# Column rings and 64-column pieces (24 KB per descriptor) in a DMA-bound grouped 1x1 convolution

## The chip, the cores and the metric

One core of a Trainium2 chip. Times are device microseconds (us) of that core.

## The reference

`x` is 512 x 512 pixels of 192 channels in bf16, in four groups of 48 channels. Each group is multiplied by its own 48 x 48 matrix:

```python
xg = x.reshape(B, H, W, G, Cg)                      # k = 1, so no padding and one tap
out = einsum('bhwgc,gcd->bhwgd', xg, w[0, 0])       # G = 4, Cg = 48
return out.reshape(B, H, W, C)                      # bf16
```

100.7 MB are read and 100.7 MB written; the arithmetic is small.

## The kernel before

Pixels are taken as 2048 columns of 128 (one pixel per partition). In one DMA each partition holds `s` neighbouring pixels, so one partition's share is one contiguous run of `s` x 384 B in memory: 12 KB at 32 columns. There are six input and six output buffers of 32 columns. The work goes in groups of 4 columns: TensorE transposes six 128 x 128 tiles into PSUM, VectorE copies them to SBUF (`ev1`), TensorE multiplies by the weights, and ScalarE copies the result to the output buffer; in every third group VectorE takes half of that (`ev2`). The code is cut, and its comments are added here:

```python
PPC = 32
HEAD = (4, 4, 8, 16)            # small pieces first, so that work starts early
TAIL = (16, 8, 4, 4)            # and last, so that it ends early
NBI = 6
NBO = 6
...
        @block.sync                                   # the load queue
        def _(sp):
            ...
            for n in range(n_chunks):
                if n >= NBI:
                    wq.wait(t_done, chunk_g1[n - NBI])        # that buffer has been transposed
                b = n % NBI
                sp.dma_start(x_sb[b][:, 0:sizes[n] * C], rows_view(xf, n)).then_inc(ld_sem[b], 16)
...
        @block.scalar                                 # ScalarE: copies, and the store queue
            def store(n):
                act.dma_start(rows_view(of, n), o_sb[b][:, 0:sizes[n] * C]).then_inc(st_sem[b], 16)
            for g in range(NG):
                n, lg = groups[g]
                if lg == 0:
                    wait_out_free(wq, n)                      # the store of n - 6 has landed
                wq.wait(mm_done, g + 1)
                while pending and pending[0][1] <= g:         # two groups after the last copy
                    store(pending.pop(0)[0])
                ...                                           # the copy of group g
```

TensorE's steady groups are a loop (`pe.Fori`); the other engines' programs are written out.

Of the kernel before, what the change touches and what calls it, by code (L numbers as in the profile page):

```python
# [6 lines left out]
BF16 = mybir.dt.bfloat16  # L7
# [14 lines left out]
ESHIFT = 112  # L22
ECOLS = 272

PPC = 32
HEAD = (4, 4, 8, 16)
TAIL = (16, 8, 4, 4)
NBI = 6
NBO = 6
NXP = 4  # L30
NOB = 4
LOOK = 3
ST_DELAY = 2
RING = 6


class Waiter:
# [9 lines left out]
        self.eng.wait_ge(sem, val)  # L47


def plan_chunks(npix):  # L50
    assert npix % 512 == 0, "the pixel count must be a multiple of 512"
    cols = npix // 128
    head, tail = list(HEAD), list(TAIL)
    if cols < sum(head) + sum(tail) + PPC:
        head, tail = [], []
    mid = cols - sum(head) - sum(tail)
    first = len(head)
    full = mid // PPC
    sizes = head + [PPC] * full
    if mid % PPC:  # L60
        sizes.append(mid % PPC)
    return sizes + tail, first, full


def bass_standalone__grouped__vision_kernel(nc, x, w, out):
# [1 line left out]
    assert Cx == C and tuple(w.shape) == (1, 1, GROUPS, CG, CG)  # L67
    npix = B * H * W_

    sizes, first_full, n_full = plan_chunks(npix)  # L70
    n_chunks = len(sizes)

    xf = x.rearrange("b h w c -> (b h w) c")
    of = out.rearrange("b h w c -> (b h w) c")
    wv = w.rearrange("a b g c d -> c (a b g) d")

    col0, groups, chunk_g0, chunk_g1, c0 = [], [], [], [], 0
    for n, s in enumerate(sizes):
        col0.append(c0)
        c0 += s  # L80
        chunk_g0.append(len(groups))
        groups += [(n, lg) for lg in range(s // 4)]
        chunk_g1.append(len(groups))
    NG = len(groups)

    body = NBI * PPC // 4
    assert body % 12 == 0
    loop_g0 = chunk_g0[first_full]
    reps = max(0, (n_full * PPC // 4 - LOOK) // body)
    loop_g1 = loop_g0 + reps * body  # L90

    def shared(g):
        return g % 3 == 1 and g < NG - 3

    dve_prog = [("wcopy", 0)]
    for g in range(NG + LOOK):
# [3 lines left out]
        if 0 <= h < NG and shared(h):  # L100
            dve_prog.append(("ev2", h))

    def rows_view(ap, n):
        s = sizes[n]
        return ap[128 * col0[n]:128 * (col0[n] + s), :].rearrange("(p i) c -> p (i c)", p=128)

    with ExitStack() as es:
        block = es.enter_context(nc.Block())
        x_sb = [es.enter_context(nc.sbuf_tensor(f"x_sb{i}", [128, PPC * C], BF16)) for i in range(NBI)]
        o_sb = [es.enter_context(nc.sbuf_tensor(f"o_sb{i}", [128, PPC * C], BF16)) for i in range(NBO)]  # L110
        xT_sb = [es.enter_context(nc.sbuf_tensor(f"xT_sb{i}", [128, 2 * UC], BF16)) for i in range(NXP)]
        ident = es.enter_context(nc.sbuf_tensor("ident", [128, 128], BF16))
        esel = es.enter_context(nc.sbuf_tensor("esel", [CG, ECOLS], BF16))
# [5 lines left out]
        def sem(name):  # L119
            return es.enter_context(nc.semaphore(name))  # L120

        ld_sem = [sem(f"ld{i}") for i in range(NBI)]
        st_sem = [sem(f"st{i}") for i in range(NBO)]
        w_sem, id_sem, e_sem, wb_sem, wc_sem = (sem(s) for s in ("w_sem", "id_sem", "e_sem", "wb_sem", "wc_sem"))
        p0_sem, p1_sem = sem("p0_sem"), sem("p1_sem")
        t_done, mm_done = sem("t_done"), sem("mm_done")
# [1 line left out]
        fa_sem = [sem(f"fa_{i}") for i in range(RING)]  # L128
        d2_sem = [sem(f"d2_{i}") for i in range(2)]

        def wait_out_free(wq, n):
            wq.wait(st_sem[n % NBO], 16 * (n // NBO))

        @block.gpsimd
        def _(gp):
# [11 lines left out]
        @block.sync  # L147
        def _(sp):
            wq = Waiter(sp)
            sp.dma_start(w_sb[:], wv).then_inc(w_sem, 16)  # L150
            for n in range(n_chunks):
                if n >= NBI:
                    wq.wait(t_done, chunk_g1[n - NBI])
                b = n % NBI
                sp.dma_start(x_sb[b][:, 0:sizes[n] * C], rows_view(xf, n)).then_inc(ld_sem[b], 16)  # L155

        @block.tensor
        def _(pe):

            def build_weights():  # L160
                pe.wait_ge(e_sem, 1)
                pe.wait_ge(w_sem, 16)
                last = None
                for (tc, r, g, c0_) in WBLOCKS:
                    s0 = ESHIFT - r
                    col = WOFF[tc] + c0_
                    last = pe.matmul(o_ps[:, NOB - 1, col:col + CG], lhsT=esel[:, s0:s0 + 128],  # L167
                                     rhs=w_sb[:, g, :], start=True, stop=True, skip_group_check=True)
                last.then_inc(wb_sem, 1)

            def transposes(g):
                n, lg = groups[g]
                if g == 0:
                    pe.wait_ge(id_sem, 1)
                if lg == 0:
                    pe.wait_ge(ld_sem[n % NBI], 16)
                xb = x_sb[n % NBI]
                ins = []
                for ul in range(2):
                    u = lg * 2 + ul  # L180
                    for tc in range(3):
                        col = u * UC + tc * 128
                        j = ul * 3 + tc
                        ins.append(pe.transpose(xT_ps[:, g % NXP, j * 128:(j + 1) * 128],  # L184
                                                xb[:, col:col + 128], ident[:]))
                if lg == 0:
                    ins[1].then_inc(ld_sem[n % NBI], -16)
                ins[-1].then_inc(t_done, 1)

            def matmuls(g):  # L190
                xs = xT_sb[g % NXP]
                waited = [e1_sem[g % RING]]
                if g == 0:
                    pe.wait_ge(wc_sem, 1)
                if g >= 2:
                    waited.append(fa_sem[(g - 2) % RING])
                    if shared(g - 2):
                        waited.append(d2_sem[(g - 2) // 3 % 2])
                for s in waited:
                    pe.wait_ge(s, 1)  # L200
                ins = []
                for ul in range(2):
                    v = 2 * g + ul
                    for tc in range(3):
                        j = ul * 3 + tc
                        c0_, c1_ = COLR[tc]
                        ins.append(pe.matmul(o_ps[:, v % NOB, c0_:c1_], lhsT=xs[:, j * 128:(j + 1) * 128],  # L207
                                             rhs=wt[:, WOFF[tc]:WOFF[tc] + (c1_ - c0_)],
                                             start=(tc == 0), stop=(tc == 2), skip_group_check=True))
                for i, s in enumerate(waited):  # L210
                    ins[1 + i].then_inc(s, -1)
                ins[-1].then_inc(mm_done, 1)

            def step(g):
                if g + LOOK < NG:
                    transposes(g + LOOK)
                matmuls(g)

            build_weights()
            for g in range(min(LOOK, NG)):  # L220
                transposes(g)
            for g in range(loop_g0 if reps else 0):
                step(g)
            if reps:
                with pe.Fori(0, reps, 1):
                    for g in range(loop_g0, loop_g0 + body):
                        step(g)
            for g in range(loop_g1 if reps else 0, NG):
                step(g)

        @block.vector
        def _(dve):
            wq = Waiter(dve)
            for (op, g) in dve_prog:
                if op == "wcopy":
                    wq.wait(wb_sem, 1)
                    dve.tensor_copy(wt[:], o_ps[:, NOB - 1, 0:WCOLS]).then_inc(wc_sem, 1)  # L237
                    continue
                n, lg = groups[g]
                if op == "ev1":  # L240
                    wq.wait(t_done, g + 1)
                    dve.tensor_copy(xT_sb[g % NXP][:], xT_ps[:, g % NXP, 0:2 * UC]).then_inc(e1_sem[g % RING], 1)  # L242
                else:
                    wait_out_free(wq, n)
                    wq.wait(mm_done, g + 1)
                    u = lg * 2 + 1
                    v = 2 * g + 1
                    dve.tensor_copy(o_sb[n % NBO][:, u * UC:(u + 1) * UC],  # L248
                                    o_ps[:, v % NOB, 0:UC]).then_inc(d2_sem[g // 3 % 2], 1)

        @block.scalar
        def _(act):
            wq = Waiter(act)
            pending = []

            def store(n):
                b = n % NBO
                act.dma_start(rows_view(of, n), o_sb[b][:, 0:sizes[n] * C]).then_inc(st_sem[b], 16)  # L258

            for g in range(NG):  # L260
                n, lg = groups[g]
                if lg == 0:
                    wait_out_free(wq, n)
                wq.wait(mm_done, g + 1)
                while pending and pending[0][1] <= g:
                    store(pending.pop(0)[0])
                v = 2 * g
                ob = o_sb[n % NBO]
                if shared(g):
                    u = lg * 2  # L270
                    ins = act.copy(ob[:, u * UC:(u + 1) * UC], o_ps[:, v % NOB, 0:UC])  # L271
                else:
                    dst = ob[:, lg * 2 * UC:(lg + 1) * 2 * UC].rearrange("p (u c) -> p u c", u=2)
                    ins = act.copy(dst, o_ps[:, v % NOB:v % NOB + 2, 0:UC])  # L274
                ins.then_inc(fa_sem[g % RING], 1)
                if g == chunk_g1[n] - 1:
                    pending.append((n, g + ST_DELAY))
            for (n, _) in pending:
                act.wait_ge(fa_sem[(chunk_g1[n] - 1) % RING], 1)
                store(n)  # L280
            for b in range(NBO):
                cnt = len(range(b, n_chunks, NBO))
                if cnt:
                    wq.wait(st_sem[b], 16 * cnt)


# [26 lines left out]
```

## Time and profile before

| | before |
|---|---|
| time, median (range) of 4 runs | 493.42 us (493.20 to 493.61) |
| span in the profile | 492.4 us |
| TensorE, VectorE, ScalarE busy | 84%, 73%, 70% |
| DMA, mean of the span / slices 5 to 37 | 409 GB/s / 427 to 430 GB/s |
| one 32-column load, issue to landing | 39.2 us (median) |

First the page: the DMA lines of its second part (40 equal slices of the span; the digit is the share of the time in which the 16 DMA engines were busy, in tenths), the queues of the third (q1 is the load queue, q10 the store queue) and the last line of the chain of the fourth.

```profile
DMA  8999999999999999999999999999999999999663
GB/s 294 414 418 425 427 427 429 430 429 429 430 429 429 429 428 427 427 429 427 428 430 429 429 430 430 429 430 427 428 427 429 428 429 429 429 429 427 279 253 143
DMA packets 20386, 201.56 MB, mean 409 GB/s; under 512 B 2448, under 2 KB 3472, under 8 KB 4496
q1 hardware_dynamic: 10288, 100.69, 48.5%
q10 hardware_dynamic: 10080, 100.67, 48.3%
DMA x_sb<-in_x_dram 71%; PE o_ps L207 13%; PE xT_ps L184 10%; ACT o_sb L274 3%; ACTq L258 1%; SPq L155 0%; SPq L150 0%; ACTq L47 0%
```

The DMA engines have work all the time, at 427 to 430 GB/s in the middle. The Trainium skill, page "DMA: Bandwidth & Descriptors", section "Where 436 GB/s comes from", gives 435.2 GB/s as the ceiling of the fabric. The trace fits it: the middle is 1.3% below. (The same section has about 358 GB/s of HBM bandwidth per core as what binds transfers between HBM and SBUF; the 429 measured on this one core are above that.) But the last three slices have 279, 253 and 143 GB/s, and that is a clue. Next, the chain of work that ended last, in order of time (start us, length us, what).

```profile
362.35 39.55 DMA x_sb<-in_x_dram
401.94 0.51 PE xT_ps L184 x6
407.92 39.53 DMA x_sb<-in_x_dram
447.49 0.51 PE xT_ps L184 x6
453.46 28.42 DMA x_sb<-in_x_dram
```

One step from load to load is 45.5 us, and it covers six pieces (the buffer count): 7.6 us for 2 x 1.573 MB, so 414 GB/s. The engines on average move 429. Some engines run ahead of the one that the chain follows.

To see it I worked two things out from the trace; they are no views of the page. A DMA's completion is sixteen separate increments of its semaphore, one for each DMA engine. For each load, the time of the first and the sixteenth:

```
load issued at   first landing   sixteenth   spread
      12.76           33.58        37.11       3.5
     134.73          165.22       174.21       9.0
     271.31          296.89       310.80      13.9
     407.92          428.57       447.45      18.9
     453.46          458.38       481.88      23.5     (the last, 4 columns)
```

Over the 18 loads between the third and the fourth row the first landing comes every 7.32 us, the sixteenth every 7.59. I call the engine that lands last the laggard. Each piece is complete only when it has landed, and by the end it is 20 us behind.

The second: the trace has a record for every DMA packet (start, duration, queue, size; no engine number). A packet starts 3 to 4 ns before the recorded end of the one before it on its engine, and a 4-byte packet follows each eight data packets of a queue, so one engine can be followed packet by packet, back from the last packet of the run. Followed so, the laggard works from its start to 491.3 us without one gap. A packet of 1.5, 3, 6 or 12 KB takes an undisturbed engine (one that shows no extra time) 61.5, 117.5, 230.5 or 456.5 ns from start to start: 4.5 ns plus the bytes at 27.2 B/ns. The laggard's 12 KB packets are recorded at 476 to 478 ns instead of 460.

So the time is the laggard's work and almost nothing else: start, its share of the bytes at the undisturbed rate, and its extra.

### The profile page before, as it was taken

The numbers are of one execution on the slowest core, as the hardware profiler recorded it, in microseconds if no ns is written. First come the engines' busy times: TensorE is split into PE (matmuls) and PEld (weight loads), VectorE is DVE, ScalarE is ACT, GpSimd is POOL, SyncE is SP. The second block draws the span as 40 slices with busy tenths as digits, with TensorE's granted clock in tenths as the row PEclk, the third lists the DMA queues.
The fourth block names the chain that finished last, engine by engine and source line by source line (L and its number), as shares of the span: only waits on it lengthen the run. The fifth ranks groups of instructions, "written<-read, shape, count | busy, mean of one in ns | idle before, by whom it ended". The sixth has DMA issues, their size and how long they took to land.

```text
span 492.4 us, 14343 instructions
## 1 busy us (share of the span) xinstructions
PE 415.0 (84%) x6154; PEld 389.1 (79%) x6154; DVE 358.1 (73%) x683; ACT 345.6 (70%) x513; POOL 1.3 (0%) x8
## 2 busy tenths in 40 slices
PE   5999999998888888888889888888888888888953
PEld 5899999887877877878778778787787787877852
DVE  3888888876777777777778777777677777777750
ACT  2788888876766777667767676776776766766752
POOL 1000000000000000000000000000000000000000
PEclk9999999999999999999999999999999999999996
DMA  8999999999999999999999999999999999999663
GB/s 294 414 418 425 427 427 429 430 429 429 430 429 429 429 428 427 427 429 427 428 430 429 429 430 430 429 430 427 428 427 429 428 429 429 429 429 427 279 253 143
DMA packets 20386, 201.56 MB, mean 409 GB/s; under 512 B 2448, under 2 KB 3472, under 8 KB 4496
## 3 DMA queue, kind: packets, MB, share of 16 engines
q1 hardware_dynamic: 10288, 100.69, 48.5%
q10 hardware_dynamic: 10080, 100.67, 48.3%
q8 instruction: 7, 0.11, 0.1%
q14 instruction: 11, 0.09, 0.0%
HBM read 100.68 MB, written 100.66 MB: 409 GB/s over the span
## 4 chain that ended last, share of the span: by engine, by line
DMA 71%; PE 24%; ACT 3%; issue 1%; ACTq 1%; SPq 0%
DMA x_sb<-in_x_dram 71%; PE o_ps L207 13%; PE xT_ps L184 10%; ACT o_sb L274 3%; ACTq L258 1%; SPq L155 0%; SPq L150 0%; ACTq L47 0%
## 5 line engine op out<-in xcount | busy, mean ns | idle before, releaser
L242 DVE COPY xT_sb<-xT_ps 128x768 bf16<-128x768 bf16 x512 | 283.8, 555 | 114.8 <-PE xT_ps L184 109.7
L274 ACT CAST o_sb<-o_ps 128x768 bf16<-128x768 f32 x342 | 267.0, 799 | 107.9 <-PE o_ps L207 101.6
L184 PE MATMUL xT_ps<-ident,x_sb 128*128 128x128 bf16 x3072 | 257.2, 220 | 58.3 <-DMA x_sb<-in_x_dram 58.3
L207 PE MATMUL o_ps<-wt,xT_sb 128*128 128x144 bf16 (+1 forms) x3072 | 297.4, 233 | 10.4 <-ACT o_sb L274 10.1
L184 PEld LDWEIGHTS xT_ps<-ident,x_sb 128*128 128x128 bf16 x3072 | 195.0, 98 | 70.0 <-DMA x_sb<-in_x_dram 68.9
L207 PEld LDWEIGHTS o_ps<-wt,xT_sb 128*128 128x128 bf16 x3072 | 211.5, 98 | 24.5 <-issue 17.7
L271 ACT CAST o_sb<-o_ps 128x384 bf16<-128x384 f32 x170 | 81.6, 480 | 33.3 <-PE o_ps L207 24.0
L248 DVE CAST o_sb<-o_ps 128x384 bf16<-128x384 f32 x170 | 94.2, 554 | 8.1 <-PE o_ps L207 7.0
L237 DVE CAST wt<-o_ps 128x480 bf16<-128x480 f32 x1 | 0.7, 657 | 3.2 <-PE o_ps L167 3.2
L167 PE MATMUL o_ps<-w_sb,esel 48*128 48x48 bf16 x10 | 0.6, 209 | 2.6 <-DMA w_sb<-in_w_dram 2.6
L167 PEld LDWEIGHTS o_ps<-w_sb,esel 48*128 48x128 bf16 x10 | 0.4, 111 | 2.5 <-POOL esel L139 2.5
L274 ACT ACT_TABLE_LOAD x1 | 1.3, 1283 | 0.8 <-PEq L298 0.8
L139 POOL TENSOR_SCALAR_AFFINE_SELECT esel<-esel 48x272 bf16<-48x272 bf16 x1 | 0.4, 406 | 0.0
L136 POOL MEMSET esel<- 48x272 bf16 x1 | 0.3, 318 | 0.3 <-POOLq L298 0.3
L143 POOL TENSOR_SCALAR_AFFINE_SELECT ident<-ident 128x128 bf16<-128x128 bf16 x1 | 0.3, 285 | 0.0
L137 POOL MEMSET ident<- 128x128 bf16 x1 | 0.2, 198 | 0.0
L298 POOL MEMSET const-bfloat16-1.0<- 128x1 bf16 x1 | 0.1, 102 | 0.0
L298 POOL MEMSET const-uint8-127<- 128x1 uint8 x1 | 0.1, 102 | 0.0
L298 POOL MEMSET const-float32-0.0<- 128x1 f32 x1 | 0.1, 98 | 0.3 <-issue 0.3
L298 POOL MEMSET const-float32-1.0<- 128x1 f32 x1 | 0.1, 98 | 0.0
## 6 DMA issues: line engine op xcount, KB each, us to landing
x_sb<-in_x_dram SPq DMA_DIRECT2D x62, 1536.0 KB, 39.2
out_dram<-o_sb ACTq DMA_DIRECT2D x62, 1536.0 KB, 31.0
x_sb<-in_x_dram SPq DMA_DIRECT2D x2, 768.0 KB, 22.1
out_dram<-o_sb ACTq DMA_DIRECT2D x2, 768.0 KB, 11.7
x_sb<-in_x_dram SPq DMA_DIRECT2D x4, 192.0 KB, 15.5
x_sb<-in_x_dram SPq DMA_DIRECT2D x2, 384.0 KB, 19.8
out_dram<-o_sb ACTq DMA_DIRECT2D x4, 192.0 KB, 6.9
out_dram<-o_sb ACTq DMA_DIRECT2D x2, 384.0 KB, 10.2
```

The costliest lines, as they stand in the source:

```text
L136: gp.memset(esel[:], 1.0).then_inc(p0_sem, 1)
L139: gp.affine_select(out=esel[:], in_=esel[:], pattern=[[-1, ECOLS]], compare_op=AluOpType.is_equal, fill=0.0, base=ESHIFT, channel_multipli ...
L167: last = pe.matmul(o_ps[:, NOB - 1, col:col + CG], lhsT=esel[:, s0:s0 + 128], rhs=w_sb[:, g, :], start=True, stop=True, skip_group_check=True)
L184: ins.append(pe.transpose(xT_ps[:, g % NXP, j * 128:(j + 1) * 128], xb[:, col:col + 128], ident[:]))
L207: ins.append(pe.matmul(o_ps[:, v % NOB, c0_:c1_], lhsT=xs[:, j * 128:(j + 1) * 128], rhs=wt[:, WOFF[tc]:WOFF[tc] + (c1_ - c0_)], start=(tc ...
L237: dve.tensor_copy(wt[:], o_ps[:, NOB - 1, 0:WCOLS]).then_inc(wc_sem, 1)
L242: dve.tensor_copy(xT_sb[g % NXP][:], xT_ps[:, g % NXP, 0:2 * UC]).then_inc(e1_sem[g % RING], 1)
L248: dve.tensor_copy(o_sb[n % NBO][:, u * UC:(u + 1) * UC], o_ps[:, v % NOB, 0:UC]).then_inc(d2_sem[g // 3 % 2], 1)
L258: act.dma_start(rows_view(of, n), o_sb[b][:, 0:sizes[n] * C]).then_inc(st_sem[b], 16)
L271: ins = act.copy(ob[:, u * UC:(u + 1) * UC], o_ps[:, v % NOB, 0:UC])
L274: ins = act.copy(dst, o_ps[:, v % NOB:v % NOB + 2, 0:UC])
L298: nc = _bacc.Bacc("TRN2", target_bir_lowering=False, num_devices=1)
```

## The change

Intent: larger packets, so that the fixed cost of each weighs less, and buffers that are rings of 256 columns, so that pieces of any size fit. VectorE takes its half in every fourth group instead of every third, since the loop is now 64 groups. The core of the diff (cut):

```diff
-PPC = 32
-HEAD = (4, 4, 8, 16)
-TAIL = (16, 8, 4, 4)
-NBI = 6
-NBO = 6
+BIG = 64
+RCOLS = 256
+HEAD = (4, 4, 8, 16, 32)
+TAIL = (32, 16, 8, 4, 4)
-RING = 6
+RING = 8
...
-        return g % 3 == 1 and g < NG - 3
+        return g % 4 == 1 and g < NG - 3
...
-        x_sb = [es.enter_context(nc.sbuf_tensor(f"x_sb{i}", [128, PPC * C], BF16)) for i in range(NBI)]
-        o_sb = [es.enter_context(nc.sbuf_tensor(f"o_sb{i}", [128, PPC * C], BF16)) for i in range(NBO)]
+        x_sb = es.enter_context(nc.sbuf_tensor("x_sb", [128, RCOLS * C], BF16))
+        o_sb = es.enter_context(nc.sbuf_tensor("o_sb", [128, RCOLS * C], BF16))
...
-        def wait_out_free(wq, n):
-            wq.wait(st_sem[n % NBO], 16 * (n // NBO))
+        def wait_out_free(wq, g):
+            if g >= body:
+                p = store_at[g - body]
+                wq.wait(st_sem[p.key], st_val[p])
...
-                if n >= NBI:
-                    wq.wait(t_done, chunk_g1[n - NBI])
-                b = n % NBI
-                sp.dma_start(x_sb[b][:, 0:sizes[n] * C], rows_view(xf, n)).then_inc(ld_sem[b], 16)
+                wq.wait(t_done, p.g1 - body)
+                sp.dma_start(ring_view(x_sb, p), rows_view(xf, p)).then_inc(ld_sem[p.key], 16)
```

More of the change, by code (lines that the diff above doesn't have):

```diff
@@ L47, in wait, with __init__, plan_pieces @@
         self.eng.wait_ge(sem, val)
-def plan_chunks(npix):
-    assert npix % 512 == 0, "the pixel count must be a multiple of 512"
-    cols = npix // 128
-    head, tail = list(HEAD), list(TAIL)
-    if cols < sum(head) + sum(tail) + PPC:
-        head, tail = [], []
-    mid = cols - sum(head) - sum(tail)
-    first = len(head)
-    full = mid // PPC
-    sizes = head + [PPC] * full
-    if mid % PPC:
-        sizes.append(mid % PPC)
-    return sizes + tail, first, full
+class Piece:
+    def __init__(self, col, size, key):
+        self.col, self.size, self.key = col, size, key
+        self.g0, self.g1 = col // 4, (col + size) // 4
+def plan_pieces(cols, head, tail):
+    sizes = list(head) if cols >= sum(head) + sum(tail) else []
+    last = list(tail) if sizes else []
+    mid = cols - sum(sizes) - sum(last)
+    pieces, c = [], 0
+    for s in sizes + [BIG] * (mid // BIG) + ([mid % BIG] if mid % BIG else []) + last:
+        whole = s == BIG and c % BIG == 0
+        pieces.append(Piece(c, s, ("big", c // BIG % (RCOLS // BIG)) if whole else ("own", len(pieces))))
+        c += s
+    return pieces
 def bass_standalone__grouped__vision_kernel(nc, x, w, out):
@@ L68, in bass_standalone__grouped__vision_kernel @@
     npix = B * H * W_
-    sizes, first_full, n_full = plan_chunks(npix)
-    n_chunks = len(sizes)
+    cols = npix // 128
+    assert npix % 512 == 0, "the pixel count must be a multiple of 512"
+    NG = cols // 4
+    loads = plan_pieces(cols, HEAD, TAIL)
+    stores = plan_pieces(cols, HEAD, TAIL)
+    load_of = {p.g0: p for p in loads}
+    store_at = {g: p for p in stores for g in range(p.g0, p.g1)}
+    store_end = {p.g1 - 1: p for p in stores}
     xf = x.rearrange("b h w c -> (b h w) c")
@@ L75, in bass_standalone__grouped__vision_kernel @@
     wv = w.rearrange("a b g c d -> c (a b g) d")
-    col0, groups, chunk_g0, chunk_g1, c0 = [], [], [], [], 0
-    for n, s in enumerate(sizes):
-        col0.append(c0)
-        c0 += s
-        chunk_g0.append(len(groups))
-        groups += [(n, lg) for lg in range(s // 4)]
-        chunk_g1.append(len(groups))
-    NG = len(groups)
-    body = NBI * PPC // 4
-    assert body % 12 == 0
-    loop_g0 = chunk_g0[first_full]
-    reps = max(0, (n_full * PPC // 4 - LOOK) // body)
+    body = RCOLS // 4
+    assert body % RING == 0 and BIG % 4 == 0 and RCOLS % BIG == 0
+    bigs = [p for p in loads if p.key[0] == "big"]
+    loop_g0 = bigs[0].g0 if bigs else 0
+    reps = max(0, (sum(p.size for p in bigs) // 4 - LOOK) // body)
     loop_g1 = loop_g0 + reps * body
     def shared(g):
-        return g % 3 == 1 and g < NG - 3
+        return g % 4 == 1 and g < NG - 3
     dve_prog = [("wcopy", 0)]
@@ L101, in bass_standalone__grouped__vision_kernel, with rows_view, ring_view @@
             dve_prog.append(("ev2", h))
-    def rows_view(ap, n):
-        s = sizes[n]
-        return ap[128 * col0[n]:128 * (col0[n] + s), :].rearrange("(p i) c -> p (i c)", p=128)
+    def rows_view(ap, p):
+        return ap[128 * p.col:128 * (p.col + p.size), :].rearrange("(p i) c -> p (i c)", p=128)
+    def ring_view(t, p):
+        at = p.col % RCOLS
+        assert at + p.size <= RCOLS
+        return t[:, at * C:(at + p.size) * C]
     with ExitStack() as es:
         block = es.enter_context(nc.Block())
-        x_sb = [es.enter_context(nc.sbuf_tensor(f"x_sb{i}", [128, PPC * C], BF16)) for i in range(NBI)]
-        o_sb = [es.enter_context(nc.sbuf_tensor(f"o_sb{i}", [128, PPC * C], BF16)) for i in range(NBO)]
+        x_sb = es.enter_context(nc.sbuf_tensor("x_sb", [128, RCOLS * C], BF16))
+        o_sb = es.enter_context(nc.sbuf_tensor("o_sb", [128, RCOLS * C], BF16))
         xT_sb = [es.enter_context(nc.sbuf_tensor(f"xT_sb{i}", [128, 2 * UC], BF16)) for i in range(NXP)]
@@ L120, in sem @@
             return es.enter_context(nc.semaphore(name))
-        ld_sem = [sem(f"ld{i}") for i in range(NBI)]
-        st_sem = [sem(f"st{i}") for i in range(NBO)]
+        ld_sem = {k: sem(f"ld_{k[0]}{k[1]}") for k in dict.fromkeys(p.key for p in loads)}
+        st_sem = {k: sem(f"st_{k[0]}{k[1]}") for k in dict.fromkeys(p.key for p in stores)}
+        st_val, seen = {}, {}
+        for p in stores:
+            seen[p.key] = seen.get(p.key, 0) + 16
+            st_val[p] = seen[p.key]
         w_sem, id_sem, e_sem, wb_sem, wc_sem = (sem(s) for s in ("w_sem", "id_sem", "e_sem", "wb_sem", "wc_sem"))
@@ L150, in _ @@
             sp.dma_start(w_sb[:], wv).then_inc(w_sem, 16)
-            for n in range(n_chunks):
-                if n >= NBI:
-                    wq.wait(t_done, chunk_g1[n - NBI])
-                b = n % NBI
-                sp.dma_start(x_sb[b][:, 0:sizes[n] * C], rows_view(xf, n)).then_inc(ld_sem[b], 16)
+            for p in loads:
+                wq.wait(t_done, p.g1 - body)
+                sp.dma_start(ring_view(x_sb, p), rows_view(xf, p)).then_inc(ld_sem[p.key], 16)
         @block.tensor
@@ L171, in transposes @@
             def transposes(g):
-                n, lg = groups[g]
                 if g == 0:
                     pe.wait_ge(id_sem, 1)
-                if lg == 0:
-                    pe.wait_ge(ld_sem[n % NBI], 16)
-                xb = x_sb[n % NBI]
+                p = load_of.get(g)
+                if p:
+                    pe.wait_ge(ld_sem[p.key], 16)
                 ins = []
                 for ul in range(2):
-                    u = lg * 2 + ul
+                    u = g % body * 2 + ul
                     for tc in range(3):
@@ L184, in transposes @@
                         ins.append(pe.transpose(xT_ps[:, g % NXP, j * 128:(j + 1) * 128],
-                                                xb[:, col:col + 128], ident[:]))
-                if lg == 0:
-                    ins[1].then_inc(ld_sem[n % NBI], -16)
+                                                x_sb[:, col:col + 128], ident[:]))
+                if p:
+                    ins[1].then_inc(ld_sem[p.key], -16)
                 ins[-1].then_inc(t_done, 1)
@@ L197, in matmuls @@
                     if shared(g - 2):
-                        waited.append(d2_sem[(g - 2) // 3 % 2])
+                        waited.append(d2_sem[(g - 2) // 4 % 2])
                 for s in waited:
@@ L238, in _ @@
                     continue
-                n, lg = groups[g]
                 if op == "ev1":
@@ L243, in _ @@
                 else:
-                    wait_out_free(wq, n)
+                    wait_out_free(wq, g)
                     wq.wait(mm_done, g + 1)
-                    u = lg * 2 + 1
+                    u = g % body * 2 + 1
                     v = 2 * g + 1
-                    dve.tensor_copy(o_sb[n % NBO][:, u * UC:(u + 1) * UC],
-                                    o_ps[:, v % NOB, 0:UC]).then_inc(d2_sem[g // 3 % 2], 1)
+                    dve.tensor_copy(o_sb[:, u * UC:(u + 1) * UC],
+                                    o_ps[:, v % NOB, 0:UC]).then_inc(d2_sem[g // 4 % 2], 1)
         @block.scalar
@@ L254, in _, with store @@
             pending = []
-            def store(n):
-                b = n % NBO
-                act.dma_start(rows_view(of, n), o_sb[b][:, 0:sizes[n] * C]).then_inc(st_sem[b], 16)
+            def store(p):
+                act.dma_start(rows_view(of, p), ring_view(o_sb, p)).then_inc(st_sem[p.key], 16)
             for g in range(NG):
-                n, lg = groups[g]
-                if lg == 0:
-                    wait_out_free(wq, n)
+                wait_out_free(wq, g)
                 wq.wait(mm_done, g + 1)
@@ L267, in _ @@
                 v = 2 * g
-                ob = o_sb[n % NBO]
+                u = g % body * 2
                 if shared(g):
-                    u = lg * 2
-                    ins = act.copy(ob[:, u * UC:(u + 1) * UC], o_ps[:, v % NOB, 0:UC])
+                    ins = act.copy(o_sb[:, u * UC:(u + 1) * UC], o_ps[:, v % NOB, 0:UC])
                 else:
-                    dst = ob[:, lg * 2 * UC:(lg + 1) * 2 * UC].rearrange("p (u c) -> p u c", u=2)
+                    dst = o_sb[:, u * UC:(u + 2) * UC].rearrange("p (u c) -> p u c", u=2)
                     ins = act.copy(dst, o_ps[:, v % NOB:v % NOB + 2, 0:UC])
                 ins.then_inc(fa_sem[g % RING], 1)
-                if g == chunk_g1[n] - 1:
-                    pending.append((n, g + ST_DELAY))
-            for (n, _) in pending:
-                act.wait_ge(fa_sem[(chunk_g1[n] - 1) % RING], 1)
-                store(n)
-            for b in range(NBO):
-                cnt = len(range(b, n_chunks, NBO))
-                if cnt:
-                    wq.wait(st_sem[b], 16 * cnt)
+                if g in store_end:
+                    pending.append((store_end[g], g + ST_DELAY))
+            for (p, _) in pending:
+                act.wait_ge(fa_sem[(p.g1 - 1) % RING], 1)
+                store(p)
+            for p in stores:
+                if st_val[p] == seen[p.key]:
+                    wq.wait(st_sem[p.key], st_val[p])
 _INS = ['x', 'w']
```

## The prediction

> **What bounds the kernel now.** The slices of the page show the DMA share at 0.9 or more in slices 2 to 37 and 427 to 430 GB/s in the middle. The Trainium skill, page "DMA: Bandwidth & Descriptors", section "Where 436 GB/s comes from", puts the ceiling at 435.2 GB/s; this trace's plateau is 1.3% below it. TensorE (84% busy) is behind that: between 13 and 32 us, where nothing waits for loads, one group of 4 columns takes 0.82 us in the timeline; from 135 us on the chain of waits advances 6 pieces in 45.5 us, 0.95 us a group.
>
> But 0.95 us a group is 414 GB/s, not 429. The trace's semaphore landings explain it. Fifteen of the sixteen DMA engines land a 32-column load every 7.32 us, one every 7.60 us. From first to sixteenth landing a load spreads over 2.0 us early and 20 us at the end. That laggard gates every piece. In its packet records a 12 KB packet takes about 475 ns instead of 457 (start to start), and it runs without a gap until the last store at 491.3 us: the last slices (279, 253, 143 GB/s) are it, nearly alone. So time = about 2 us of start + the laggard's service of its 12.6 MB + half a microsecond.
>
> **What the change does.** Steady packets go from 12 KB to 24 KB. From start-to-start times of 61.5, 117.5, 230.5 and 456.5 ns for 1.5, 3, 6 and 12 KB, a packet costs 4.5 ns plus bytes at 27.2 GB/s. So 24 KB should take 909 ns, against twice 456.5: 0.5%. Per engine 992 12 KB packets become 480 of 24 KB and 32 of 12 KB: 480 x 4.5 = 2.2 us saved. 140 DMAs become 80: 60 completions at about 6 ns, 0.4 us.
>
> The laggard's extra 18 ns per packet doesn't look like a cost per packet: near the end its 6 KB packets show about 5 extra, 3 KB under 2, 1.5 KB none, and its 12 KB packets ran at the fast 460 while compute paused (480 to 482 us). It looks tied to bytes or to compute. I expect it to stay at 3 to 4%.
>
> Ring instead of six buffers, 256 columns against 192: deeper queues, but the queues never ran dry. VectorE's share going from every third group to every fourth costs ScalarE about 0.03 us a group, off the path. Coarser stores (15 us of work each) may turn waits of TensorE for loads into waits of ScalarE for output space; no matter while the laggard stays busy. At the end each small load packet alternates with a 24 KB store packet; I estimate 0 to 4 us in which the laggard may idle while the last groups are computed.
>
> **Predicted:** 493.6 - 2.6 + about 1 = 492 us; 8 in 10 between 487 and 497. Faster by over 2%: 0.06; within 2%: 0.90; slower: 0.04.
>
> **What would show it.** About 11,600 packets instead of 20,386; 24 KB packets near 912 ns; plateau 430 to 432 GB/s; the landings still spreading, by about 0.5 us per 64 columns; the laggard busy to within a microsecond of the end. Median load landing above 45 us.
>
> **What would make it wrong.** If the laggard's extra is per packet, it halves: 8 us more saved, about 483. If 24 KB packets take more than twice 456.5, or their pitch upsets memory, slower. If the laggard idles longer in the tail, up to 500.

## The result, and the profile after

| | before | after |
|---|---|---|
| time, median (range), 4 runs each | 493.42 us (493.20 to 493.61) | 491.66 us (491.26 to 491.83) |
| ratio (95% interval) | 1 | 0.9963 (0.9946 to 0.9981) |
| span in the profile | 492.4 us | 489.8 us |
| TensorE, VectorE, ScalarE busy | 84%, 73%, 70% | 86%, 69%, 73% |
| mean granted TensorE clock in the profile | 0.989 | 0.956 |

A ratio is the mean time of one kernel's runs over that of the other's in the same rounds, so it is not quite the ratio of the medians. The granted clock of TensorE is lower after the change. By the chains, DMA and not TensorE is what ends last in both kernels, and the laggard's extra doesn't follow the clock: in the runs below it is 14.1 us at 0.904 (copy_pe) and 14.6 us at 1.0 (copy_pe_small). The same lines of the page after:

```profile
DMA  8999999999999999999999999999999999998593
GB/s 297 430 425 423 428 430 433 427 435 425 436 425 432 433 431 433 429 432 431 425 433 430 429 435 429 434 429 433 429 429 426 438 421 434 421 424 351 238 385 149
DMA packets 11750, 201.63 MB, mean 412 GB/s; under 512 B 1488, under 2 KB 2512, under 8 KB 3536
q1 hardware_dynamic: 5968, 100.68, 48.3%
q10 hardware_dynamic: 5760, 100.67, 48.2%
DMA out_dram<-o_sb 73%; PE o_ps L215 10%; PE xT_ps L192 8%; DMA x_sb<-in_x_dram 4%; ACT o_sb L277 1%; SPq L164 0%; ACTq L264 0%; SPq L161 0%; ACTq L46 0%
```

Packets fall from 20,386 to 11,750. The recorded 24 KB packet takes 912 ns (the median over all engines), which is what 4.5 ns plus the bytes at 27.2 B/ns gives. The rate in the middle, by the view of windows (100 to 400 us), is 431 GB/s against 429. The same slow end is there (351, 238, 385, 149): the laggard is still behind. The chain is now of stores instead of loads, and so are the waits (engine and what it waited for: us in total, times, longest us), first before, then after:

```profile
PE xT_ps L184 <- DMA x_sb<-in_x_dram: 58.3, 54, 3.2
...
```

```profile
ACT o_sb L277 <- DMA out_dram<-o_sb: 46.9, 23, 2.8
DVE o_sb L255 <- DMA out_dram<-o_sb: 26.7, 22, 1.9
PE xT_ps L192 <- DMA x_sb<-in_x_dram: 7.3, 4, 3.9
...
```

TensorE waited 58.3 us for loads before and waits 7.3 us after; ScalarE waits 46.9 us and VectorE 26.7 us for output space instead. The DMA issues (KB each, median us from issue to landing), before and then after, say the same: the load is now the one that lands early, the store the one that waits.

```profile
x_sb<-in_x_dram SPq DMA_DIRECT2D x62, 1536.0 KB, 39.2
out_dram<-o_sb ACTq DMA_DIRECT2D x62, 1536.0 KB, 31.0
```

```profile
x_sb<-in_x_dram SPq DMA_DIRECT2D x30, 3072.0 KB, 25.7
out_dram<-o_sb ACTq DMA_DIRECT2D x30, 3072.0 KB, 45.4
```

The reason lies in the first 60 us. In the packet records of one engine, load and store packets alternate one by one while both queues have work. The 40 small store packets of the head (4 to 32 columns) then each let a 24 KB load packet through, so loads get ahead (86% of the laggard's bytes between 25 and 50 us are loads, 57% before). Later the output ring is what is full. That the size of the pieces does this and not the rings is shown by piece32 below, which has the same rings with 32-column pieces: no wait there is for output space, and TensorE waits for loads again.

```profile
PE xT_ps L192 <- DMA x_sb<-in_x_dram: 64.0, 53, 3.2
```

The change of waits costs nothing: the laggard has work either way, and its packets follow one another without a gap to the last one at 489.0 us.

So what the change is worth must be read from the laggard alone. I summed, over the packets followed, what each takes from start to start, and split it into what a packet of that size takes an undisturbed engine and the rest, the extra. The first packets of a run can't be told apart from the other engines'; they were filled in from the missing bytes. So the split between start and extra is soft; their sum, 22.7 us before and 22.8 us after, is not.

```
laggard, us        start   undisturbed work   extra   last packet ends
before              3.5         468.7          19.2         491.3
after               2.6         466.2          20.2         489.0
difference         -0.9          -2.5          +1.0          -2.4
```

The predicted saving of packets and completions (2.6 us) is there: 2.5 us. The column of undisturbed work is computed from packet counts and undisturbed times, so it holds whatever the extra does; whether it reaches the time is for the runs below to show. Two other terms came out otherwise than told: the extra grew by a microsecond, and the start took 0.9 us less. The growth is real: between 60 and 420 us, where nothing was filled in, the extra is 13.3 us before and 14.7 after (15.1 in after_again; 12.6 and 12.8 in piece32 and piece32_again). The earlier start may not be the change's: the profile before is of an execution of 494.27 us, slower than all four timed ones, the profile after of an ordinary one (491.59 us).

### The profile page after: what moved, and what is told of

Its sections match the earlier page's. It is cut to its first block, busy times and chain, and to the rows that moved or that the text cites. A ratio compares the mean times of both kernels' runs of the same rounds, so it can differ in the third digit from the quotient of the medians.

```text
span 489.8 us, 14171 instructions
## 1 busy us (share of the span) xinstructions
PE 423.4 (86%) x6154; PEld 407.9 (83%) x6154; DVE 336.1 (69%) x640; ACT 357.2 (73%) x513; POOL 1.3 (0%) x8
## 4 chain that ended last, share of the span: by engine, by line
DMA 77%; PE 18%; ACT 1%; another core or an unknown queue 1%; issue 1%; SPq 1%; ACTq 0%
DMA out_dram<-o_sb 73%; PE o_ps L215 10%; PE xT_ps L192 8%; DMA x_sb<-in_x_dram 4%; ACT o_sb L277 1%; SPq L164 0%; ACTq L264 0%; SPq L161 0%; ACTq L46 0%
## 5 line engine op out<-in xcount | busy, mean ns | idle before, releaser
L277 ACT CAST o_sb<-o_ps 128x768 bf16<-128x768 f32 x385 | 301.7, 799 | 116.8 <-PE o_ps L215 68.4
L215 PE MATMUL o_ps<-wt,xT_sb 128*128 128x144 bf16 (+1 forms) x3072 | 308.2, 238 | 47.9 <-ACT o_sb L277 44.8
L192 PE MATMUL xT_ps<-ident,x_sb 128*128 128x128 bf16 x3072 | 265.7, 225 | 7.8 <-DMA x_sb<-in_x_dram 7.3
L215 PEld LDWEIGHTS o_ps<-wt,xT_sb 128*128 128x128 bf16 x3072 | 217.8, 100 | 61.4 <-issue 52.5
L192 PEld LDWEIGHTS xT_ps<-ident,x_sb 128*128 128x128 bf16 x3072 | 205.6, 101 | 9.5 <-DMA x_sb<-in_x_dram 7.6
L255 DVE CAST o_sb<-o_ps 128x384 bf16<-128x384 f32 x127 | 69.8, 550 | 28.0 <-DMA out_dram<-o_sb 26.7
L274 ACT CAST o_sb<-o_ps 128x384 bf16<-128x384 f32 x127 | 61.0, 480 | 8.0 <-PE o_ps L215 5.1
## 6 DMA issues: line engine op xcount, KB each, us to landing
x_sb<-in_x_dram SPq DMA_DIRECT2D x30, 3072.0 KB, 25.7
out_dram<-o_sb ACTq DMA_DIRECT2D x30, 3072.0 KB, 45.4
x_sb<-in_x_dram SPq DMA_DIRECT2D x4, 192.0 KB, 27.2
```

Source lines behind the costliest of these rows:

```text
L192: ins.append(pe.transpose(xT_ps[:, g % NXP, j * 128:(j + 1) * 128], x_sb[:, col:col + 128], ident[:]))
L215: ins.append(pe.matmul(o_ps[:, v % NOB, c0_:c1_], lhsT=xs[:, j * 128:(j + 1) * 128], rhs=wt[:, WOFF[tc]:WOFF[tc] + (c1_ - c0_)], start=(tc ...
L255: dve.tensor_copy(o_sb[:, u * UC:(u + 1) * UC], o_ps[:, v % NOB, 0:UC]).then_inc(d2_sem[g // 4 % 2], 1)
L274: ins = act.copy(o_sb[:, u * UC:(u + 1) * UC], o_ps[:, v % NOB, 0:UC])
L277: ins = act.copy(dst, o_ps[:, v % NOB:v % NOB + 2, 0:UC])
```

## The experiments

The theory: one DMA engine has an extra that comes from what the compute engines do, not from the packets; the change therefore saves only the packets' fixed cost, times what that engine carries. The rivals for the extra: that engine has a byte rate of its own (25.9 B/ns was seen with both packet sizes), or pays per packet. Runs on one chip share the runs of the kernel before: copy_only, piece32, pool_flood and split2; then copy_pe, copy_pe_small and copy_act_dve; then copy_pe_loop, after_again, piece32_again and piece128; then copy_pe32 alone.

### copy_only: no computing

The edit, cut: the programs of GpSimd, TensorE and VectorE and ScalarE's copies go, and a load waits for the stores that last read its place in the ring.

```diff
+        @block.scalar
+            for p in stores:
+                wq.wait(ld_sem[p.key], ld_val[p.col])
+                act.dma_start(rows_view(of, p), ring_view(x_sb, p)).then_inc(st_sem[p.key], 16)
-RCOLS = 256
+RCOLS = 512
```

> Wrong result on purpose: no computing, the same loads of x and the same stores, from the buffer that was loaded. Theory (the slowest DMA engine is slowed by what the compute engines do): with them silent, the spread from first to sixteenth landing stays at 2 to 3 us to the end, every engine takes 14.54 us per 64 columns, and the time is about 2 + 32 x 14.54 + 3 = 470 us. Rival (that engine has a byte rate of its own, 25.9 GB/s): the spread grows by 0.6 us per piece to 20 us, and the time is 487 to 490 us.

Measured (result wrong on purpose): 473.56 us (472.53 to 474.02, 4 runs), ratio 0.959 to the kernel before. The page:

```profile
span 472.2 us, 119 instructions
DMA  8999999999999999999999999999999999999998
GB/s 301 431 424 428 436 433 433 433 433 433 431 431 433 433 433 433 433 433 433 433 433 433 429 433 431 433 433 433 433 433 433 433 433 431 433 428 426 443 429 332
```

433 GB/s to the end: no slow tail. One engine fell 6.6 us behind in the first 60 us, with long packets at the start, and stayed there; the packets of all sixteen engines together show 0.5 us of extra from 60 us on, where the laggard alone has 16.6 us of it between 60 and 450 us in the changed kernel. So the byte rate is not the engine's own, and the cost is not per packet: both rivals fall. The extra is caused by computing.

### pool_flood: more instructions

```diff
+            for k in range(60):
+                if k:
+                    gp.wait_ge(f_sem, 64 * k)
+                for i in range(64):
+                    gp.memset(junk[:, i:i + 1], 0.0).then_inc(f_sem, 1)
```

> The changed kernel, correct, with 3840 memsets of one column on GpSimd beside it, 27% more instructions. If the slowest DMA engine is slowed by the number of instructions, whatever they move: its extra of about 0.6 us per 64 columns grows by a quarter, 495 to 497 us. If it is slowed by the data that TensorE, ScalarE and VectorE move: 491.7 us.

Measured: correct, 496.43 us (496.17 to 496.71, 4 runs), ratio 1.0062 to the kernel before, against 0.9975 and 0.9963 for the changed kernel. The size is as told, but it isn't a clean proof. The flood was over at 162 us. An engine was 17 us behind at 127 us and did not fall further back later; another engine, which I take for the usual laggard, caught up with it at the end (the fifteenth and sixteenth landings of the last load are 1.7 us apart, 481.0 and 482.7 us). And the written-out memsets have to be fetched, which the DMA engines do too:

```profile
q14 instruction: 40, 0.33, 0.2%
q14 instruction: 10, 0.08, 0.0%
```

(The first line is this run's, the second the changed kernel's.) In the packet records 31 fetches of 8 KB at 309 ns or more, 10.5 us in all, fall into the flood. If they all ran on that engine, which no record shows, fetching explains most of this lag, so the next runs have no such fetches.

### copy_pe, copy_pe_small, copy_act_dve: one engine's work beside the DMA

The DMA-only kernel of copy_only, with one engine's instructions on constants beside it. copy_pe:

```diff
+        @block.tensor
+            with pe.Fori(0, 8, 1):
+                for g in range(64):
+                    ...   # six transposes of 128 x 128 and six matmuls of 144 or 192 columns
```

copy_pe_small:

```diff
-                    ...   # six transposes of 128 x 128 and six matmuls of 144 or 192 columns
+                    for n in range(12):
+                        pe.matmul(o_ps[0:2, n % NOB, 0:2], lhsT=cst[:, 0:2], rhs=cst[:, 0:2],
+                                  start=True, stop=True, skip_group_check=True)
```

copy_act_dve (rings of 448 columns, to make room):

```diff
+            for k in range(512):                                # VectorE
+                dve.tensor_copy(xT_sb[k % NXP][:]..., o_ps[:, 2:4, 0:UC]).then_inc(v_sem, 1)
+                    act.copy(a_sb[made % 4]..., o_ps[:, 0:2, 0:UC]).then_inc(a_sem, 1)   # ScalarE, 512 times
```

> Wrong result on purpose: the DMA-only kernel with TensorE running beside it, 12288 transposes and matmuls with their weight loads of the sizes of the kernel, on constants, waiting for nothing; ScalarE and VectorE silent. If what slows one DMA engine comes from TensorE: one engine lags by 15 to 19 us in all while TensorE runs (about 385 us), and the time is 485 to 490 us instead of 473.6. If it comes from ScalarE and VectorE: 474 us and no growing lag.

> Wrong result on purpose: the same, but each matmul has two columns of weights and two of data, so as many TensorE instructions that move almost nothing. If the number of TensorE instructions counts: again 15 to 19 us of lag on one engine, 485 to 490 us. If what they read and write counts: 474 us.

> Wrong result on purpose: the DMA-only kernel with 512 ScalarE and 512 VectorE copies of 128 x 768 from PSUM to SBUF, as much as the kernel moves there, TensorE silent. If TensorE's instructions are the cause: 474 us, no engine lags by more than 3 us. If the traffic of ScalarE and VectorE is the cause: 485 to 490 us.

Measured: 486.18, 485.85 and 476.55 us. Their outputs are wrong, which doesn't matter for the times. Lines of the page of copy_pe_small, then of copy_act_dve:

```profile
PE   6459999999999910000000000000000000000000
GB/s 305 425 425 427 426 441 424 424 437 428 426 433 433 426 430 439 430 426 443 428 428 439 430 428 439 433 426 439 433 428 435 435 430 428 441 425 430 432 333 54
```

```profile
DVE  9999999999999999999999999999999999999600
ACT  7999999989767797777986778877779777794300
GB/s 300 431 427 436 442 431 433 431 431 431 432 431 432 433 433 431 431 433 433 433 432 435 434 431 435 431 435 431 431 430 431 432 431 433 435 435 421 429 429 264
```

With TensorE the slow tail is back (332 or 333, then 54 GB/s), with two-column matmuls just as with full ones. With ScalarE and VectorE busy and moving about as much as the kernel moves, it is not (429, 264). They aren't quite without effect: the spread of a store's landings grows from 2.1 us at 28 us to 4.5 us at the end, more than the 3 us that were told, with the last three engines apart from the rest and from each other, and the time is 2.5 us over 473.6. The timing inside copy_pe_small is the sharpest sign. TensorE ends at 171 us there. The laggard's 24 KB packets, recorded ns, mean:

```
                       TensorE running          TensorE done
                       loads    stores          loads    stores
copy_pe                926.1     971.8          912.0     914.9
copy_pe_small          957.8    1073.9          912.0     912.3
```

By the view of windows TensorE does 40.1 small matmuls per us (4407 in 110 us) and 16.0 of the full ones (5124 in 320 us), 2.5 times as many. The extra of a load and a store packet is 10.2% of their time (207.7 of 2031.7 ns) against 3.9% (73.9 of 1897.9 ns), 2.6 times as much. In all it is the same, 14.6 us against 14.1. The extra goes with the number of TensorE instructions that are executed (12,288 in both, half of them weight loads, which these runs don't tell apart), about 1.2 ns each, and not with what they move. These matmuls update no semaphore, so a semaphore isn't needed for it.

This is most of the laggard's extra and not all of it: the full kernels execute 12,308 TensorE instructions, and the extra is 19 to 20 us there instead of 14 to 15. No run here tells where the other 5 us come from; the full kernels' instructions also wait for and update semaphores, and the other engines work beside them.

### copy_pe_loop: is it the fetching of TensorE's instructions?

```diff
-            with pe.Fori(0, 8, 1):
-                for g in range(64):
+            with pe.Fori(0, 512, 1):
+                if True:
```

> Wrong result on purpose: the DMA-only kernel with the small TensorE instructions, but as 512 turns of a loop of 12 matmuls instead of 8 turns of 768. If the traffic that slows one DMA engine is the fetching of TensorE's instructions, and a loop that small is not fetched again: no lag, 474 us. If each executed instruction costs whatever its place (its recording, for instance): 486 us again, with about 12 us more lag on one engine.

Measured (one look): 488.29 us, extra 15.0 us. The lag is the same for a loop of 12 matmuls. (The time is 2.4 us over copy_pe_small's mostly because of the start: followed as above, the laggard has done 5.8 us of its undisturbed work by 12 us, and 8.9 us in copy_pe_small.) The page's list of queues has no instruction queue in this run, copy_pe_small's has 6 packets of it, the last at 41 us, while its lag grows to the end of TensorE's work at 171 us. First copy_pe_loop's queues, then the line of copy_pe_small:

```profile
q1 hardware_dynamic: 5760, 100.67, 48.5%
q10 hardware_dynamic: 5760, 100.67, 48.3%
```

```profile
q8 instruction: 6, 0.10, 0.1%
```

So it is not the fetches that the trace records. What would fit is something that goes out once for every executed TensorE instruction and meets one DMA engine, such as the profiler's own record of each instruction. No run here shows it, since all were profiled; it stays open, and with it whether the laggard exists without the profiler.

### piece32, after_again, piece32_again: the packet size alone

piece32 and piece32_again are one kernel; after_again is the changed kernel once more.

```diff
-BIG = 64
-HEAD = (4, 4, 8, 16, 32)
-TAIL = (32, 16, 8, 4, 4)
+BIG = 32
+HEAD = (4, 4, 8, 16)
+TAIL = (16, 8, 4, 4)
```

> The changed kernel with steady pieces of 32 columns, 12 KB packets again; ring, VectorE's share of every fourth group and the rest stay. If the 0.4% comes from the packet size: 493 us, like the kernel before, fast engines at 7.32 us per 32 columns. If it comes from the ring or the sharing: 491.7 us.

> The changed kernel, for comparison on the same chip: ratio 0.996 to the kernel before.

> The changed kernel with 32-column pieces, 12 KB packets, more rounds. If the gain is the packets' fixed cost: ratio 1.000 to the kernel before, 0.4% over the changed kernel on this chip. If it is the ring and the sharing: like the changed kernel.

| | median (range), runs | ratio to before (95%) |
|---|---|---|
| piece32 | 494.89 us (492.34 to 495.81), 4 | 1.0035 (0.9999 to 1.0071) |
| piece32_again | 494.18 us (492.11 to 494.89), 6 | 1.0016 (0.9998 to 1.0033) |
| after_again | 491.97 us (491.90 to 492.41), 6 | 0.9975 (0.9962 to 0.9988) |
| before, beside the last two | 493.27 us (492.44 to 494.51), 11 | 1 |

The ring and the sharing gain nothing; all of the gain goes with the larger pieces, that is, with 24 KB packets and fewer DMAs. But the two kernels with 12 KB packets spread over 2 to 3.5 us on these chips and the changed one over 0.5. And the profiles, which fell on quick executions of them (492.34 and 492.11 us), show why one look would have misled:

```
laggard, us        undisturbed work   extra   last packet ends
piece32                 468.8          18.1         489.3
piece32_again           468.7          17.8         489.1
after_again             466.1          20.8         489.3
```

The 2.6 us of packets are there again, and in this pair of executions the extra gave all of them back.

### copy_pe32: does the packet size change the extra?

copy_pe with the three lines of piece32's diff.

> Wrong result on purpose: DMA with TensorE beside it as before, but 12 KB packets. The slow engine's packets without the extra should sum to 2.5 us more than with 24 KB. If its extra per TensorE instruction is the same for both packet sizes: extra again 14.1 us, time about 488.5 us. If 24 KB packets make the extra larger, as the profiles of the full kernels suggest (18 to 19 against 20 to 21 us): extra 12 to 13 us and a time within a microsecond of the 486.2 us of 24 KB.

Measured (one look): 489.08 us against 486.18 of copy_pe. The laggard's undisturbed work is 468.7 us against 466.1, its extra 14.3 against 14.1. Here the packet saving of 2.6 us comes through whole (the times differ by 2.9 us, though these are on two chips) and the extra doesn't depend on the packet size. So the larger extra of the full kernel with 24 KB packets is not a property of the packets beside TensorE alone. Its cause stays open.

### piece128: 48 KB packets

```diff
-BIG = 64
-HEAD = (4, 4, 8, 16, 32)
-TAIL = (32, 16, 8, 4, 4)
+BIG = 128
+HEAD = (4, 4, 8, 16, 32, 64)
+TAIL = (64, 32, 16, 8, 4, 4)
```

> The changed kernel with 128-column pieces, 48 KB packets, two to a ring. By the fixed cost alone a further 1.1 us less than the changed kernel, about 490.5; but only two pieces fit each ring, so loads are issued when 128 columns are used up and the last store is late: if a queue runs dry, 495 to 510 us.

Measured: correct, 502.44 us (499.71 to 503.31, 6 runs), ratio 1.0172. The page and two of its waits:

```profile
DMA  8999999998999999999999997999999999998697
GB/s 309 449 374 445 416 390 430 429 412 376 350 424 427 432 431 376 435 439 432 392 388 431 420 401 314 404 428 424 431 365 389 439 437 427 403 433 375 261 429 327
ACT o_sb L277 <- DMA out_dram<-o_sb: 29.1, 9, 6.7
PE xT_ps L192 <- DMA x_sb<-in_x_dram: 28.1, 9, 7.8
```

With two pieces to a ring the queues do run dry: several slices of 314 to 392 GB/s where the changed kernel has 421 to 438 throughout, and both kinds of wait at once, for loads and for output space. So the further 1.1 us of the fixed cost was not had with two pieces to a ring.

### split2: giving the laggard less

```diff
+SPLIT = (640, 1408)
+CUT = 120
...
-                act.dma_start(rows_view(of, p), ring_view(o_sb, p)).then_inc(st_sem[p.key], 16)
+                dst, src = rows_view(of, p), ring_view(o_sb, p)
+                for a, b in ((0, CUT), (CUT, 128)) if p.col in SPLIT else ((0, 128),):
+                    act.dma_start(dst[a:b], src[a:b]).then_inc(st_sem[p.key], 16)
```

> The changed kernel, correct, but two of the 30 big stores go in two DMAs, partitions 0 to 119 (eight for each of fifteen engines, if so divided) and 120 to 127 (one for each of eight). If the slowest engine is the one that then gets nothing: it saves 2 x 8 x 0.95 = 15 us, its lag falls back by 7 us at each of the two, and the time is 476 to 481 us. If it is another engine: 491 to 494 us and the spread grows as before.

Measured: correct, 503.06 us (502.50 to 503.42, 4 runs), ratio 1.0193: neither outcome. The spread of a store's landings goes from 6 us before the first split store to 25 to 29 us after it (33 to 40 after the second), so many engines were thrown apart, not one relieved. The mean recorded 24 KB store packet rose from 918.6 to 939.6 ns over all engines, with single ones of 3.9 us. The division was as meant: the store queue has 654 completion packets, 38 x 16 + 2 x (15 + 8), which is what the Trainium skill's page "DMA: Bandwidth & Descriptors", section "Why a DMA increments its semaphore by 16 and not by 1", makes of 120 and 8 partitions (the largest number up to 16 that divides them). Why it throws the engines apart the trace doesn't tell, so this says nothing of which engine the laggard is, and evening out its load is left untried.

## Why the prediction was right

The time: 492.0 told, 491.66 measured, "within 2%" at 0.90.

- "Time = about 2 us of start + the laggard's service + half a microsecond": right. The laggard works without a gap in both kernels, and the whole difference of 2.4 us in its last packet is in its own work and start.
- "4.5 ns plus bytes at 27.2 GB/s", so "2.2 us saved" and "60 completions, 0.4 us": right. 24 KB packets take 912 ns, and the laggard's undisturbed work, counted with these times, fell by 2.5 us (2.6 in copy_pe32 against copy_pe, and in after_again against piece32_again). In the time of whole runs it shows as 2.2 us between after_again and piece32_again, and as 2.9 us between copy_pe and copy_pe32.
- "The laggard's extra doesn't look like a cost per packet ... tied to bytes or to compute": right, and the experiments narrow it to compute, and for about 14 of its 19 to 20 us to TensorE's executed instructions. Byte rate is ruled out by copy_only.
- "I expect it to stay at 3 to 4%": a little low. 19.2 of 468.7 us is 4.1% before, and 20.2 and 20.8 of 466 are 4.3 and 4.5% after. This term was taken as unchanged and is +1 us (in the profile beside 12 KB pieces on the other chip, +3 us).
- "0 to 4 us in which the laggard may idle" at the end, about 1 in the sum: it was 0. That the extra grew by about the microsecond that was set down for this idling is luck: the right size on the wrong term. The landings of the last four loads were far apart, but store packets filled the time.
- The start came out 0.9 us earlier in the profiles, which was not in the sum. The profiles' difference of 2.4 us is larger than that of the medians, 1.8 us, since the profile before is of a slow execution; the total of 1.6 us (493.6 to 492.0) is nearer to the 1.8 than the wrong terms let one expect.
- "Coarser stores may turn waits of TensorE for loads into waits of ScalarE for output space; no matter": right, 58.3 us against 46.9 us of them, and no time moved.
- "Median load landing above 45 us": wrong. It is 25.7 us, and the store's is 45.4. I had counted the deeper input ring and not asked what the larger pieces do: as loads got ahead in the head, the output ring became the one that is full, and loads were issued later. With the ring and 12 KB packets (piece32) the median is 54.5 us, as the deeper ring alone would have it.

## What to carry to other kernels

When DMA bounds a kernel, ask which engine ends last: a mean rate of 429 GB/s hid one engine at 414 that set the time, and it is told by comparing the chain's rate with the mean rate and by a slow last tenth of the span. A change is then worth what it takes off that engine; 24 KB packets instead of 12 KB took off 0.5% of its work. With 48 KB packets only two pieces fitted a ring; the queues ran dry, and it was 1.7% slower than the kernel before. Four pieces to a ring were enough, three were not tried. All runs were profiled, so look first whether your kernel has a laggard without the profiler, if you can.

## What the Trainium skill lacked or had wrong

- "DMA: Bandwidth & Descriptors", section "Latency and other measured facts", says that engines 7 and 15 are usually slower and guesses at the descriptor rings of DMAs issued from GpSimd. Here no data DMA is issued from GpSimd, and one of the sixteen engines was still 4% slower. The laggard of the runs with TensorE alone lost 14 to 15 us to 12,288 executed TensorE instructions, about 1.2 ns each, whatever they moved; with no compute the sixteen engines together lost 0.5 us from 60 us on. (The trace doesn't number the engines, and all runs were profiled.)
- The same page, section "Why small descriptors are slow (HBM only)", has a fixed cost of about 3 cycles per packet. With the 850 MHz of the same page's ceiling that is 3.5 ns, an estimate. From 1.5 to 24 KB these runs show 4.5 ns per packet plus the bytes at 27.2 B/ns.
- The same page, "Why a DMA increments its semaphore by 16 and not by 1", tells how many engines a DMA of 120 partitions uses, but not at what price: two stores of 40 done as 120 and 8 partitions instead of 128 cost about 11 us (503.06 us against 491.97 on another chip; 1.0193 against 0.9975 of the kernel before).
- "Runtime: NRT & Kernel Launch", section "Instruction fetch mechanics", gives 16 KiB blocks. The traces show packets of 16 KB on one instruction queue (q8), about 880 to 1,000 ns each for most, and of 8 KB on the other (q14), 309 ns each for most.
- "DMA: Bandwidth & Descriptors", section "Queues, rings and completion order", has an engine take turns between queues by packets of typically 9 to 17 descriptors. The records here alternate one by one, load and store, at 12 and at 24 KB each (the 4-byte packet after eight data packets takes a turn too), and a 1.5 KB store takes turns with a 24 KB load.
